# Block-sorted attention and a squared-ReLU FFN: half of the first q loaded in fp32 by SyncE and cast by ScalarE, with a new order of the work

## The chip, the cores and the metric

One core of a Trainium2 chip runs the whole kernel. The metric is the device time of one execution in microseconds; the median of three runs of the kernel before is 220.72 us (220.32 to 221.7).

## What is computed

There are 4 batches, 8 heads, 768 tokens and a head dimension of 64. The tokens of a head form 8 blocks of 96. A Sinkhorn iteration makes an 8x8 matrix P for each head, P mixes the blocks of k and of v, each block of q attends to its own mixed block, and a feed-forward layer follows.

```python
P = sort_net
for _ in range(5):
    P = exp(P - max(P, -1)); P = P / sum(P, -1); P = P / sum(P, -2)
k_sorted = einsum('bhij,bhjcd->bhicd', P, k_blocks)      # the same for v
attn = softmax(q_block @ k_sorted_block.T / sqrt(D))     # 96x96, block by block
x = (attn @ v_sorted_block)  as [3072 tokens, 512]
h = max(x @ w_in, 0)                                     # 512 -> 2048
out = (h * h) @ w_out                                    # 2048 -> 512
```

All inputs and the output are fp32; the kernel computes in bf16 with fp32 sums.

## The kernel before

**Stages.** A pair of heads (`hp`, 0 to 3) of a batch is one unit of attention, and half a batch (384 tokens) is one unit of the FFN, eight in all. A unit of attention goes through K and V (the sorts: k and v times the spread P, L593 and L629, evicted by L248 and L250), S (scores L664, then exp L684 or L693), T (a transpose of v, L713), A (product with v L855, then a reciprocal and a multiply on DVE, L865 and L866) and X (a transpose of the result into xT: on PE, L914, or as a DMA transpose on SP, L890). Batch 0 is done in two halves, so that the first FFN unit can begin early. An FFN unit is 64 up matmuls (L983; six of unit 0's are made ahead as single pieces, L941), a ReLU on ACT (L991), a square on DVE (L994), and 48 down matmuls (L1013, L1041) whose results go out through L962 on SP.

**Loads.** GpSimd (POOL) issues all loads of q, k, v and the weights, in one stream, and its DMAs turn fp32 into bf16 on the way (L320). Batch 0 comes first: all heads of q in two pieces of 64 partitions each (L351, L352), then k and v in turn for each pair, then w_in, w_out, and batch 1. SP loads only sort_net (L265). Batches 2 and 3 are loaded behind small copies on POOL (`hold`, L1130) that wait for xT of the batch before.

**The lead-in.** While the loads come, ACT and DVE run the five Sinkhorn rounds: an exp on ACT (L441), then sums, reciprocals and products on DVE (L398 to L402). PE runs matmuls on a tile of ones that nobody reads (`fill`, L427), 10 of them at the start (`warm`, L431), and others where the planner sees a gap. Between them PE transposes q of batch 0 (L543), and ACT copies the results into qT (L248); these copies stand in ACT's queue between the exps. At the end of the rounds p is spread over the partitions (L454), w_all is built from it (L466, on DVE and POOL), and the sorts begin.

**What sets the order.** The kernel writes its order by hand. Every step is an `Op` with an engine, a cost in us and its dependencies. `Plan.run` (L136) goes through them with these costs, and the instructions are recorded in the order that comes out; each engine runs its own in order. Two lists steer it: `FIRST` gives the order on PE for the first half of batch 0 (K0, v0 and so on; F0 to F7 are the FFN pieces made ahead; capitals are evicted by ACT, small letters by DVE, and a quote switches the PSUM buffer), and `DUES` gives, for each later step of attention, the number of FFN steps after which it is due on PE. DMA transfers are Ops of the pseudo-engines DMA and WAY, whose costs stand for the time on the way.

**v by way of DRAM.** From batch 1 on, v is sorted in another layout (L749), cast to `vn`, written to the DRAM buffer v_way by SP (L773) and read back as `vblk` (L779). k and q are turned by DMA transposes on SP (kx, L804; qz, L831). The DMA transposes of the second half of batch 0 (L890) wait for a POOL copy, the `gate` (L896), that waits for part 2 of w_out.

Of the kernel before, what the change touches and what calls it, by code (L numbers as in the profile page):

```python
# [8 lines left out]
FP32 = mybir.dt.float32  # L9
BF16 = mybir.dt.bfloat16  # L10
AF = mybir.ActivationFunctionType
ALU = mybir.AluOpType
# [6 lines left out]


DUES = {
    (0, "K"): (-266.0, -275.0, -427.5, -387.5),
    (0, "S"): (-233.0, -241.5, -349.0, -343.5),
    (0, "T"): (-217.0, -257.5, -368.5, -320.5),
    (0, "A"): (-107.5, -204.5, -291.0, -102.0),
    (0, "X"): (-11.0, -68.5, -149.5, -90.5),
    (0, "W"): (-274.5,),
    (1, "V"): (-104.0, -85.5),
    (1, "Q"): (-75.0,),
    (1, "N"): (None, -22.5),  # L30
    (1, "Z"): (None, None, -13.5, 11.0),
    (1, "S"): (-49.5, 0.0, 8.5, 49.0),
    (1, "A"): (-13.0, 2.0, 11.0, 50.5),
    (1, "X"): (42.0, 19.0, 38.5, 54.0),
    (2, "L"): (42.0,),
    (2, "N"): (57.5, 84.5),
    (2, "V"): (63.5, 76.0),
    (2, "Z"): (73.0, 73.0, 98.0, 88.0),
    (2, "S"): (90.5, 92.5, 100.5, 99.5),
    (2, "A"): (92.0, 93.5, 101.5, 100.0),  # L40
    (2, "X"): (99.0, 107.0, 110.0, 107.5),
    (3, "L"): (117.5,),
    (3, "N"): (122.5, 135.0),
    (3, "V"): (130.5, 141.0),
    (3, "Z"): (138.5, 146.5, 155.5, 153.5),
    (3, "S"): (148.5, 150.0, 161.5, 158.5),
    (3, "A"): (149.5, 154.0, 161.5, 159.5),
    (3, "X"): (155.5, 159.5, 236.5, 162.0),
}

FIRST = ("K0' v0 K1 v1 S0 t0 S1 t1' A0 K2 V2 A1 K3 S2 t2 v3 S3 x1 A2 T3' x0' A3 X2 F0 F1 F4 F6 "
         "F7 x3 F3")


class Op:
# [127 lines left out]
def kernel(  # L185
# [10 lines left out]
    nc = tc.nc  # L196
# [110 lines left out]
    w_in_bf = const.tile([128, KC, d_ff], BF16)  # L307
    w_out_bf = const.tile([128, NT, d_model], BF16)
    xT = const.tile([128, KC, n_tok], BF16)
    w_all = const.tile([128, H + HP, NB, C0], BF16)  # L310
    w_t = const.tile([128, NH // 4, 4, NB], BF16)
    qkv = {}
# [35 lines left out]

    first = plan.add("DMA", 4.55, lambda e: None)
    landed["last"] = first  # L350
    load(0, 0, 0, H, slice(0, 64))  # L351
    load(0, 0, 0, H, slice(64, 128))  # L352
    id_op = plan.add("POOL", 0.4, lambda e: make_identity(nc, ident, nomemset=True))
    mask = const.tile([128, C0], BF16)
    mask_t = const.tile([128, 4], BF16)
# [67 lines left out]
    def fill(us, slot):  # L423

        n = int(us / 0.24)
        for r in [4] * n + [2] * (us - 0.24 * n > 0.12):
            nc.tensor.matmul(  # L427
                out=p2[slot][:, 0, 0:128 * r].rearrange("p (r x) -> p r x", r=r), lhsT=ones,
                rhs=ones[:, None, :].to_broadcast([128, r, 128]), start=True, stop=True)

    def warm(e):  # L431
        fill(2.4, 0)


    plan.add("PE", 4.3, warm, [plan.add("DVE", 1.1, lambda e: None)])

    exps = []
    step = plan.add("SP", 2.25, lambda e: None)
    step0 = step
    for it in range(5):  # L440
        step = plan.add("ACT", 0.26, lambda e: nc.scalar.activation(  # L441
            out=p_sb, in_=p_sb, func=AF.Exp), [step])
        exps.append(step)
        if it == 0:
            plan.add("ACT", 0.6, make_sel, [step, id_op])
        step = plan.add("DVE", 0.66, lambda e: sink_norm(e, 0), [step])
        step = plan.add("DVE", 0.47 if it == 4 else 0.72, lambda e, it=it: sink_norm(e, 1, it == 4), [step])

# [81 lines left out]
    def s_q(b, hp, p0, p1, due=0, after=None, eng=AD):  # L530

        n = p1 - p0
        t = {}

        def mm(e):
            qb = qkv[b][0]
            if b == 0:
                t["p"] = psf.tile([128, NA, n], BF16, tag="pf", name="qtp")
            else:
                t["p"] = ps1.tile([128, NA, n], BF16, tag="p1", name="qtp")  # L540
            for a in range(NA):
                for h in range(2):
                    nc.tensor.transpose(  # L543
                        out=t["p"][64 * h:64 * (h + 1), a, :],
                        in_=qb[p0:p1, 2 * hp + h, D * a:D * (a + 1)],
                        identity=ident[p0:p1, p0:p1])
# [12 lines left out]

        if b == 0:  # L560
            dep = landed[b, 0, 0, p0]
        else:
            dep = landed[b, 0, HP * (2 * hp // HP), 0]
        ring = rf if b == 0 else r1
        s1, old = ring.take()
        if p0 == 0:
            qTs[b, hp], oldq = rqT.take()
        else:
            oldq = []
        pe = plan.add("PE", 0.04 + 0.0023 * n, mm, [dep, id_op] + old, due, mode="col")  # L570
# [314 lines left out]
    def s_xt(u, due=0, eng=AD, own=True):  # L885
        early = u.b == 0 and u.halves == (1,) and u.hp < HP - 1
        if early or u.b > 1 or u.b == 1 and u.hp < HP - 1:
            def turn(e):
                t0 = S * u.b + BLK * u.i0
                nc.sync.dma_start_transpose(  # L890
                    out=xT[:, u.hp, t0:t0 + BLK * u.ni].rearrange("p (n q) -> p n q", q=BLK),
                    in_=u.ao.rearrange("p n e d -> p (n e d)"))

            if early and "gate" not in holds:
                def gate(e):
                    nc.gpsimd.tensor_copy(out=xT[0:1, 0:HP - 1, HS:HS + 1],  # L896
                                          in_=w_out_bf[0:1, 3 * NT // 4 - HP + 1:3 * NT // 4, 0:1])

                holds["gate"] = plan.add("POOL", 0.1, gate, [landed["w_out", 2]])
            sp = plan.add("SP", 1.4, turn, u.norms + [holds["gate"]] * early)  # L900
            op = plan.add("WAY", 6.0 if early else 1.3, lambda e: None, [sp], tail=5.0 if early else None)
            rao.use(u.nao, op)
            for hf in u.halves:
                x_done[u.b, u.hp, hf] = op
            return
        st = {}

        ring = r1 if own else rf

# [281 lines left out]
```

## Time and profile before

| What | Value |
|---|---|
| median of 3 runs | 220.72 us |
| the profiled execution, its own time | 221.3 us |
| its span | 219.5 us |
| PE busy | 210.1 us (96%) |
| ACT, DVE, POOL busy | 120.8, 109.0, 28.5 us |
| up matmuls L983 | 506, 326 ns each |
| down matmuls L1013 | 352, 379 ns each |
| DMA | 31.52 MB, mean 144 GB/s |

The span is the time from the first to the last instruction in the profile. A row of the timeline gives the start and the duration in us, the engine, the line, the operation, out<-in and the count, and in brackets how long the engine sat idle before and what released it. PE is the matmul row and PEld the load of its weights. Matmuls are pipelined, so one shows 326 ns where the next follows after 163.

### The profile page before, as it was taken

To read this page: it belongs to the slowest core of one execution; us is meant where nothing else is said; L and a number is where in the kernel's file an instruction comes from. 1 tells how busy PE (TensorE), PEld (TensorE's weight loads), DVE (VectorE), ACT (ScalarE), POOL (GpSimd) and SP (SyncE) were. 2 spreads that over 40 slices of the span, in tenths; PEclk is the share of its full clock that TensorE was granted. 3 is DMA by queue.
4 is the path that set the end of the run, shared out by engine and by line. 5 is a ranking of instruction groups with operands and counts; after the bars stand their busy time and mean duration, and the time that the engine had idled before them with its cause. 6 is when DMAs were issued, how large, how long until landed. Compare 5 with 4: busy or idle time off the path is not lost.

```text
span 219.5 us, 5063 instructions
## 1 busy us (share of the span) xinstructions
PE 210.1 (96%) x2020; PEld 115.7 (53%) x2036; DVE 109.0 (50%) x298; ACT 120.8 (55%) x248; POOL 28.5 (13%) x53
## 2 busy tenths in 40 slices
PE   8998999979999999999989999999999999999994
PEld 2566765436555555445645455445655465456542
DVE  5777764245687437327666136426694155015300
ACT  4675885236875268326974168426866276147421
POOL 7994221000000510000000150000000000000000
PEclk9999999999999999999999999999999999999999
DMA  5999999999784599369974489689987310120012
GB/s 65 198 202 207 207 207 212 184 174 268 198 165 113 75 216 225 52 172 187 203 196 85 134 138 226 116 206 203 154 205 110 97 48 3 48 88 7 0 51 96
DMA packets 47831, 31.52 MB, mean 144 GB/s; under 512 B 27264, under 2 KB 42880, under 8 KB 47808
## 3 DMA queue, kind: packets, MB, share of 16 engines
q0 software_dynamic: 12736, 13.63, 38.5%
q1 hardware_dynamic: 35072, 17.56, 34.9%
q8 instruction: 16, 0.26, 0.5%
q14 instruction: 7, 0.06, 0.1%
HBM read 29.70 MB, written 8.72 MB: 175 GB/s over the span
## 4 chain that ended last, share of the span: by engine, by line
PE 79%; DMA 12%; POOL 4%; issue 1%; ACT 1%; DVE 1%; SPq 0%; POOLq 0%
PE hp L983 36%; PE op L1013 31%; DMA xT<-ao 5%; DMA w_in_bf<-in_moe_w_in_dram 5%; PE p L855 3%; PE p L664 3%; DMA vblk<-v_way 3%; PE op L1041 2%; PE p L749 1%; POOL kb L320 1%; POOL vb L320 1%; ACT h L991 1%; PE p L629 1%; DVE h L994 1%; PE hp L941 1%
## 5 line engine op out<-in xcount | busy, mean ns | idle before, releaser
L983 PE MATMUL hp<-xT,w_in_bf 128*128 128x384 bf16 x506 | 88.2, 326 | 1.5 <-DMA xT<-ao 1.5
L1013 PE MATMUL op<-w_out_bf,h 128*128 128x512 bf16 x352 | 82.9, 379 | 0.9 <-issue 0.2
L991 ACT ACTIVATE h<-hp 128x384 bf16<-128x384 f32 x128 | 62.1, 494 | 19.0 <-PE hp L983 16.2
L994 DVE TENSOR_TENSOR h<-h 128x384 bf16<-128x384 bf16 x128 | 43.8, 355 | 48.5 <-ACT h L991 48.1
L983 PEld LDWEIGHTS <-w_in_bf 128*128 128x128 bf16 x506 | 47.2, 98 | 33.3 <-DMA xT<-ao 2.0
L1013 PEld LDWEIGHTS <-h 128*128 128x128 bf16 x368 | 34.1, 98 | 38.0 <-issue 0.9
L248 ACT COPY ob<-op 128x512 f32<-128x512 f32 (+2 forms) x25 | 14.2, 568 | 50.6 <-PE op L1013 48.2
L693 ACT ACTIVATE et<-p 96x384 bf16<-96x384 f32 x48 | 19.9, 488 | 8.5 <-PE p L664 8.2
L866 DVE TENSOR_TENSOR ao<-p,rec 96x512 bf16<-96x512 f32 x32 | 22.0, 686 | 1.1
L855 PEld LDWEIGHTS <-et 96*128 96x128 bf16 x256 | 11.4, 97 | 6.5 <-ACT h L991 1.7
L865 DVE RECIPROCAL rec<-p 96x8 f32<-96x8 f32 x32 | 6.4, 202 | 13.0 <-PE p L855 12.1
L250 DVE CAST vn<-p 128x768 bf16<-128x768 f32 x6 | 5.7, 958 | 13.3 <-PE p L749 13.3
L1130 POOL COPY held<-xT 1x3 bf16<-1x3 bf16 (+1 forms) x2 | 0.4, 184 | 85.6 <-DMA xT<-ao 85.6
L855 PE MATMUL p<-vblk,et 96*128 96x65 bf16 x192 | 9.6, 193 | 1.3 <-DMA vblk<-v_way 1.3
L809 DVE COPY kvT<-kx 128x768 bf16<-128x768 bf16 x10 | 8.5, 848 | 4.7 <-DMA kx<-kn 4.7
L427 PE MATMUL p<-ones 128*128 128x512 bf16 (+1 forms) x28 | 9.3, 459 | 1.3 <-DVE ones L269 1.1
L664 PEld LDWEIGHTS <-kvT 64*128 64x128 bf16 x256 | 6.3, 94 | 5.9 <-issue 1.9
L248 ACT CAST vn<-p 128x768 bf16<-128x768 f32 x6 | 4.8, 799 | 5.9 <-PE p L749 5.9
L250 DVE CAST kn<-p 128x768 bf16<-128x768 f32 x5 | 4.8, 958 | 6.0 <-PE p L749 6.0
L320 POOL DMA_DIRECT2D kb<-in_k_dram x10 | 6.4, 644 | 4.4 <-DMA w_in_bf<-in_moe_w_in_dram 2.0
L320 POOL DMA_DIRECT2D vb<-in_v_dram x10 | 6.3, 632 | 4.0 <-DMA w_in_bf<-in_moe_w_in_dram 4.0
L320 POOL DMA_DIRECT2D qb<-in_q_dram x8 | 6.2, 770 | 4.6 <-DMA w_out_bf<-in_moe_w_out_dram 2.1
(80 smaller groups left out, 114.9 us busy)
## 6 DMA issues: line engine op xcount, KB each, us to landing
out_dram<-ob SPq DMA_DIRECT2D x23, 256.0 KB, 3.4
qb<-in_q_dram POOLq DMA_DIRECT2D x8, 384.0 KB, 11.7
v_way<-vn SPq DMA_DIRECT2D x6, 396.0 KB, 5.1
vblk<-v_way SPq DMA_DIRECT2D x6, 396.0 KB, 4.2
vb<-in_v_dram POOLq DMA_DIRECT2D x6, 384.0 KB, 12.0
kb<-in_k_dram POOLq DMA_DIRECT2D x6, 384.0 KB, 10.6
w_in_bf<-in_moe_w_in_dram POOLq DMA_DIRECT2D x4, 512.0 KB, 12.2
w_out_bf<-in_moe_w_out_dram POOLq DMA_DIRECT2D x4, 512.0 KB, 17.6
```

The source lines that it names most:

```text
L248: nc.scalar.copy(out=out, in_=in_)
L250: nc.vector.tensor_copy(out=out, in_=in_)
L320: nc.gpsimd.dma_start(out=dst, in_=src)
L427: nc.tensor.matmul(out=p2[slot][:, 0, 0:128 * r].rearrange("p (r x) -> p r x", r=r), lhsT=ones, rhs=ones[:, None, :].to_broadcast([128, r, ...
L664: nc.tensor.matmul(out=scp[:, h, BLK * n:BLK * (n + 1)], lhsT=u.ksT[64 * h:64 * (h + 1), HS * hf + BLK * n:HS * hf + BLK * n + 128], rhs=( ...
L693: nc.scalar.activation(out=et[:, h, 0:HS].rearrange("p (n c a) -> p n c a", c=C0, a=NA), in_=st["p"][0:96, h, 0:HS].rearrange("p (n a c) - ...
L855: nc.tensor.matmul(out=oup[:, h, 66 * n:66 * n + D + 1], lhsT=et_r[u.et[hf]][:, h, BLK * n:BLK * n + 128], rhs=(u.vs[:, NQ * hf + n, h, 0: ...
L866: nc.vector.tensor_tensor(out=u.ao[:, n0:n0 + NQ, :, :].rearrange("p n e d -> p e n d"), in0=ov[:, :, :, 0:D], in1=rec[:, :, :, None].to_b ...
L983: nc.tensor.matmul(out=t["hp", nt][:, 0:HS], lhsT=w_in_bf[:, kc, 128 * nt:128 * (nt + 1)], rhs=xT[:, kc, t0:t0 + HS], start=(kc == 0), sto ...
L991: nc.scalar.activation(out=t["h1", nt], in_=t["hp", nt][:, 0:HS], func=AF.Relu)
L994: nc.vector.tensor_tensor(out=t["h2"][:, nt, :], in0=t["h1", nt], in1=t["h1", nt], op=ALU.mult)
L1013: nc.tensor.matmul(out=t["op", mt], lhsT=t["h2"][:, nt, 128 * mt:128 * (mt + 1)], rhs=w_out_bf[:, nt, :], start=(nt == 0), stop=(nt == NT ...
```

## The change

q of heads 0 to 3 of batch 0 is no longer loaded by POOL. SP loads it in fp32, in two DMAs of two heads, right after sort_net, into a part of xT that is not yet used. ACT casts each into qb, behind exps 1 and 2. POOL's two q loads carry heads 4 to 7 only. The transposes of pairs 0 and 1 wait for the casts. Four instructions on constants are new, ahead of the fill on PE (two fp32 matmuls), on DVE (one multiply with a running sum, with a memset before it and a reciprocal after it) and on ACT (an exp whose scale is read from a tile). No output depends on them. All entries of `DUES` and the order in `FIRST` are new, and the time that the planner keeps a DMA transpose of xT in the second half of batch 0 busy on the way changes (`tail` from 5.0 to 3.8).

```diff
-    (0, "K"): (-266.0, -275.0, -427.5, -387.5),
+    (0, "K"): (-232.0, -238.5, -413.0, -404.5),
...
-    (1, "V"): (-104.0, -85.5),
-    (1, "Q"): (-75.0,),
+    (1, "V"): (-107.5, -57.0),
+    (1, "Q"): (-50.0,),
...
-FIRST = ("K0' v0 K1 v1 S0 t0 S1 t1' A0 K2 V2 A1 K3 S2 t2 v3 S3 x1 A2 T3' x0' A3 X2 F0 F1 F4 F6 "
-         "F7 x3 F3")
+FIRST = ("K0 v0 k1' S0 t0' v1 K2' k3 S1 A0 T1' V2' v3 S2 A1 T2' t3' S3 x0' A2 X1 F0 F1 A3 X2 F3 "
+         "F4 x3 F6 F7")
...
+    q32 = [xT[:, 1 + g, 2 * S:].bitcast(FP32).rearrange("p (h x) -> p h x", h=2)
+           for g in range(2)]
+    for g in range(2):
+        nc.sync.dma_start(out=q32[g], in_=q_r[0, :, 2 * g:2 * g + 2, :])
...
-    load(0, 0, 0, H, slice(0, 64))
-    load(0, 0, 0, H, slice(64, 128))
+    load(0, 0, HP, HP, slice(0, 64))
+    load(0, 0, HP, HP, slice(64, 128))
...
+    t32 = xT[:, 3, 2 * S:].bitcast(FP32)
+    nc.vector.memset(t32[:, 0:128], 1.0)
+    nc.vector.scalar_tensor_tensor(
+        out=t32[:, 128:136], in0=t32[:, 0:8], scalar=1.0, in1=t32[:, 8:16],
+        op0=ALU.mult, op1=ALU.mult, accum_out=t32[:, 136:137])
+    nc.vector.reciprocal(out=t32[:, 137:138], in_=t32[:, 136:137])
+
     def warm(e):
+        for n in (8, 16):
+            nc.tensor.matmul(out=p2[1][:, 0, 16 * n:17 * n], lhsT=t32[:, 0:128],
+                             rhs=t32[:, 0:n], start=True, stop=True)
         fill(2.4, 0)
 
+    def try_exp(e):
+        nc.scalar.activation(out=t32[:, 140:148], in_=p2[1][:, 0, 128:136], func=AF.Exp,
+                             scale=t32[:, 137:138])
...
         if it == 0:
+            plan.add("ACT", 0.4, try_exp, [step])
+        if it == 1:
             plan.add("ACT", 0.6, make_sel, [step, id_op])
+        if it in (1, 2):
+            def cast(e, g=it - 1):
+                alloc_qkv(0)
+                nc.scalar.copy(out=qkv[0][0][:, 2 * g:2 * g + 2, :], in_=q32[g])
+
+            casts.append(plan.add("ACT", 0.8, cast, [step, plan.add(
+                "WAY", 2.6 + 0.9 * it, lambda e: None, tail=2.6 + 0.9 * it)]))
...
-            dep = landed[b, 0, 0, p0]
+            dep = casts[hp] if hp < HP // 2 else landed[b, 0, HP, p0]
...
-            op = plan.add("WAY", 6.0 if early else 1.3, lambda e: None, [sp], tail=5.0 if early else None)
+            op = plan.add("WAY", 6.0 if early else 1.3, lambda e: None, [sp], tail=3.8 if early else None)
```

More of the change, by code (lines that the diff above doesn't have):

```diff
@@ L21 @@
 DUES = {
-    (0, "K"): (-266.0, -275.0, -427.5, -387.5),
[L23 to L27, printed above, removed]
-    (1, "V"): (-104.0, -85.5),
-    (1, "Q"): (-75.0,),
[L30 to L48, printed above, removed]
-}
-FIRST = ("K0' v0 K1 v1 S0 t0 S1 t1' A0 K2 V2 A1 K3 S2 t2 v3 S3 x1 A2 T3' x0' A3 X2 F0 F1 F4 F6 "
-         "F7 x3 F3")
+    (0, "K"): (-232.0, -238.5, -413.0, -404.5),
+    (0, "S"): (-204.0, -204.5, -355.5, -296.0),
+    (0, "T"): (-231.5, -163.5, -378.0, -266.0),
+    (0, "A"): (-198.0, -109.5, -291.0, -100.5),
+    (0, "X"): (-51.5, -27.5, -263.5, -74.5),
+    (0, "W"): (-288.5,),
+    (1, "V"): (-107.5, -57.0),
+    (1, "Q"): (-50.0,),
+    (1, "N"): (None, -39.5),
+    (1, "Z"): (None, None, 1.0, 47.5),
+    (1, "S"): (-40.5, -15.5, 11.5, 49.5),
+    (1, "A"): (-27.5, 2.5, 12.5, 51.5),
+    (1, "X"): (22.0, 6.0, 42.5, 54.5),
+    (2, "L"): (45.5,),
+    (2, "N"): (70.5, 75.5),
+    (2, "V"): (73.0, 79.0),
+    (2, "Z"): (79.5, 85.0, 93.5, 93.0),
+    (2, "S"): (80.0, 85.5, 99.5, 97.0),
+    (2, "A"): (80.0, 87.5, 101.0, 98.5),
+    (2, "X"): (89.5, 99.0, 125.0, 130.0),
+    (3, "L"): (130.5,),
+    (3, "N"): (130.5, 138.5),
+    (3, "V"): (132.0, 143.0),
+    (3, "Z"): (142.5, 143.0, 153.0, 145.0),
+    (3, "S"): (148.0, 148.5, 161.0, 157.0),
+    (3, "A"): (148.0, 156.5, 162.5, 157.5),
+    (3, "X"): (155.5, 165.0, 169.0, 183.5),
+}
+FIRST = ("K0 v0 k1' S0 t0' v1 K2' k3 S1 A0 T1' V2' v3 S2 A1 T2' t3' S3 x0' A2 X1 F0 F1 A3 X2 F3 "
+         "F4 x3 F6 F7")
 class Op:
@@ L429, in fill @@
                 rhs=ones[:, None, :].to_broadcast([128, r, 128]), start=True, stop=True)
+    t32 = xT[:, 3, 2 * S:].bitcast(FP32)
[4 more added lines that the diff above has]
+    nc.vector.reciprocal(out=t32[:, 137:138], in_=t32[:, 136:137])
     def warm(e):
+        for n in (8, 16):
+            nc.tensor.matmul(out=p2[1][:, 0, 16 * n:17 * n], lhsT=t32[:, 0:128],
+                             rhs=t32[:, 0:n], start=True, stop=True)
         fill(2.4, 0)
+    def try_exp(e):
+        nc.scalar.activation(out=t32[:, 140:148], in_=p2[1][:, 0, 128:136], func=AF.Exp,
+                             scale=t32[:, 137:138])
     plan.add("PE", 4.3, warm, [plan.add("DVE", 1.1, lambda e: None)])
-    exps = []
+    exps, casts = [], []
     step = plan.add("SP", 2.25, lambda e: None)
```

## The prediction

> **What bounds the kernel now.** I read the page first, then the waits of PE, the chain of work in order of time, the timeline of the first 23 us, and the windows of the same stretch.
>
> ```profile
> PE 210.1 (96%) x2020; PEld 115.7 (53%) x2036; DVE 109.0 (50%) x298; ACT 120.8 (55%) x248; POOL 28.5 (13%) x53
> ```
> PE is busy for 210.1 of 219.5 us, so only what PE waits for, or what stands before its useful work, can be won. The waits of PE (total, times, longest) name two stalls after the lead-in:
> ```profile
> PE hp L983 <- DMA xT<-ao: 1.5, 1, 1.5
> PE p L855 <- DMA vblk<-v_way: 1.3, 1, 1.3
> ```
> The chain (start, us, what) places them:
> ```profile
> 10.43 9.93 DMA w_in_bf<-in_moe_w_in_dram
> 20.36 0.05 issue
> 20.41 0.50 PE hp L941 x2
> ...
> 22.72 1.08 PE hp L983 x6
> ...
> 38.07 11.39 DMA xT<-ao
> 49.46 0.05 issue
> 49.51 2.12 PE hp L983 x12
> ...
> 110.04 5.55 DMA vblk<-v_way
> ```
> From 22.72 on PE does the same work in both kernels. So the end is: the time of that milestone (first L983, its six L941 pieces done), plus fixed work, plus stalls. The opening timeline (start, us, engine, line) shows what sets the milestone:
> ```profile
> 1.06 5.58 PE L427 MATMUL p<-ones 128*128 128x512 bf16 x15 [1.06 <-DVE ones L269]
> 1.25 1.52 POOL L320 DMA_DIRECT2D qb<-in_q_dram  x2 [0.80 <-POOLq L1175]
> 6.98 0.48 ACT L248 COPY qT<-qtp 128x384 bf16<-128x384 bf16 x1 [0.91 <-PE qtp L543]
> 7.58 0.26 ACT L441 ACTIVATE p_sb<-p_sb 32x64 f32<-32x64 f32 x1
> 16.17 0.27 PEld L593 LDWEIGHTS <-kb 128*64 128x64 bf16 x12 [0.35 <-DMA kb<-in_k_dram]
> 17.64 0.27 PEld L593 LDWEIGHTS <-vb 128*64 128x64 bf16 x12 [0.60 <-DMA vb<-in_v_dram]
> ```
> The sorts of pair 3 wait for kb at 16.17 and vb at 17.64, the first FFN piece for w_in at 20.41: until the milestone the load stream decides. Windows (DMA share and GB/s last) show when it starts:
> ```profile
> 3.50:4.00 0.50, 0.50 (x2) 0.15 (x1) 0.43 (x3) 0.31 (x1) 0.48 (x2) 1.00 0.55 48
> 4.00:4.50 0.50, 0.50 (x3) 0.20 (x2) 0.18 (x2) 0.26 (x1) 0.42 (x2) 1.00 1.18 177
> ```
> It is at speed only from about 4.0, and then holds about 200 GB/s of bf16, which is 0.4 MB of fp32 a microsecond.
>
> **What the Trainium skill says.** "DMA: Bandwidth & Descriptors", section "Issuing engines are not separate DMA queues": all issuers share the same 16 engines and another one saves issue time only. So the move buys an earlier start, not a higher rate; the trace of before agrees in so far as its stream is flat once it runs. "TensorE: Matmul & The Clock Gate", Part 1: the array runs at 1.2 GHz until about 3.4 us of sustained work, with N=512 matmuls 426.7 ns apart. The trace agrees on the pitch: weight loads of the fill stand 0.43 us apart up to 5.72. "FP8 and Floating Point Precision", TensorE Precision Notes: a true FP32 product takes four passes. No fp32 matmul is in this trace.
>
> **The change, part by part.**
>
> *Loads.* Half of q (4 heads, 4*128*384*4 B = 0.786 MB) leaves POOL's queue for SP's, right behind p_sb, whose issue at 0.74 took 0.40; p_sb landed 1.5 us after its issue. I put the first q bytes at 2.5 (estimate), and 0.786/0.4 = 2.0 us for them, so 4.5 for the end. Before, the same bytes went over 4.0 to 6.0. The rest of the stream moves up by 1.5 us. Lower bound 0 (same engines, slow start for HBM itself), upper 2.0 (all of it free). POOL still issues two q pieces, only of half the size, so its queue of k, v and weights issues when it did (kb 3.08, vb 5.43): early enough, as 1.573 MB of q last until 2.5+3.9 = 6.4. Arrivals become kb3 14.7, vb3 16.1, w_in 18.9.
>
> *Casts.* Two ACT casts of 128x768; nearest row, the 128x768 cast of vn: 0.80. ACT runs exps at 2.29, 4.05, 5.81, 7.58, 9.34, and between them is idle. Cast 0 goes behind sel: 4.31+0.62+0.80 = 5.73, just ahead of 5.81; cast 1 is 6.07 to 6.9. Cover: the DVE half of each Sinkhorn round. Both cost nothing while q has landed; behind them in ACT's queue stand exps 2 and 3, and so the whole Sinkhorn chain.
>
> *Trial instructions.* On DVE a memset, a scalar_tensor_tensor and a reciprocal, under 0.2 each by the rows of their neighbours, inside the 0.85 idle before 2.58: nothing. On ACT one Exp (0.26) in idle time before 4.05: nothing. On PE two fp32 matmuls stand ahead of all fill and wait for the last memset (et ends 1.73, this one about 1.9) in place of the first: PE starts 0.85 later. Their price is unknown. Below: two short bf16 ones, 0.1. Above: four passes with a weight load that reads four times as long, 2*4*0.43 = 3.4. I take eight passes of a cold load at 0.13 each: 1.0. Fill then starts near 2.9 instead of 1.06. The planner was not told (its costs for the fill are unchanged): in the program's order PE has 11 fills before the first q transposes, 4 behind them, and some 24.5 before the spread of p, against 24 now. With 11 fills at 0.43 (the last ones faster if the clock is up) the first transposes come at about 7.4, the ACT copy of qT at 7.8, and exp 3, which stands behind it, at 8.3 instead of 7.58. Exp 4 waits likewise for three more copies. The spread, now at 11.32, slips by about 0.8 (0 to 1.6).
>
> *Lead-in with the new order.* I walk K0 to X3 with durations of the rows: sort 0.2 (+0.4 to its eviction), ACT copy 0.48, exp 0.81, DVE copy 0.56, norm 0.9, T copies 0.42/0.58. With the spread on time: K0 12.03, S0 exp 13.4, K2 copy 14.5 (POOL's w_all is done at 14.05, behind its w_in issues), S1 exp 15.4 (kb3 at 14.7 stands ahead of S1 on PE), T1 16.2, V2 16.8, S2 exp 17.3, T2 18.1, S3 exp 18.7 to 19.5, A3 norm 20.1 to 21.0, X3 21.05, last pieces, 0.88 of L629 sorts: milestone 22.5. The spread 0.8 late costs only 0.1 of it, because POOL and kb3 give slack: 22.6. 1.5 late gives 23.2. I take 22.8, or +0.1, with a range of -0.2 to +0.8. So ACT, not the stream, becomes the limit, and the earlier loads are worth almost nothing here.
>
> *First stall.* The third transpose of xT was issued about 38, after a POOL gate on w_out part 2 (35.23); it now moves up with the stream by about 1.4, and lands near 48.1. In front of its user the new DUES also put 12 q transposes and 24 sorts (0.46+0.67 = 1.13). PE is then ready at 48.0+0.1+1.13 = 49.2: no wait. Gain 1.5.
>
> *Second stall.* The new order has batch 1's attention some 8 to 16 down-projection matmuls (0.22 each) earlier, so batch 2 loads earlier. The last attention product of pair 2 was at 69.2; from 48.1 I now add 1.13, 64 up-projection matmuls at 0.163 (10.4), 8 down (1.7) and about 4.0 for the k sorts, scores and products between: 65.3. The gate on the loads, 73.48 before, and all that hangs on it come some 3 us earlier. On SP the second v_way write stands one transpose earlier and the vblk read no longer behind two out_dram. The read, 110.04 before, comes at about 103 and lands near 108, and its user stands at 110. Gain 1.3. Batch 3 by the same walk keeps some 2 us of slack.
>
> *Sum.* -1.5 -1.3 +0.1 = -2.7; I keep 0.1 for waits that the walk misses: -2.6. The profiled execution took 221.3 for its span of 219.5, so span 216.9 and 218.7 for that execution. The median of the runs, 220.72, is 0.58 below the profiled one; the same 2.6 off it gives 218.1.
>
> **Rivals.**
> *One stall stays.* The vblk path has four steps (gate, load, write, read), each with its queue; if one is late, or a new wait of the size appears, only 1.5-0.1 is won: 219.4. For it: the write took up to 11.1 us to land. Against: 2 us of slack by the walk.
> *The transfer is hidden anyway.* If SP's bytes bring the stream no forward, kb3 stays at 16.2, and in the new order S1's exp stands behind it: milestone about 23.9, +1.2. Both stalls still shrink by the order: -2.8+1.2 = -1.6, or 219.1. Against: the stream idles before 4.0.
> *Slower: the fp32 pair at the head of PE.* If fill starts so late that the spread slips over 3.9 us, the milestone slips 2.9 (past 1.5 late it follows one to one) and eats both gains. With the 1.0 for 0.8 above, that needs a pair of over about 4 us; at 5, 222. Its upper price of 3.4 speaks against it. No other step holds up PE so early.
>
> **How the numbers follow.** Chances: forecast 0.60, one stall 0.18, hidden 0.15, slower 0.07. A measurement of this kernel tells about 1%, 2.2 us, from no change, so faster means under 218.5. The forecast, 217.2 to 218.9 on its own bounds, is under it 8 times in 10 (0.48); the others add 0.04: faster 0.52. Slower by over 1% only at the far end of the last: 0.05. Same 0.43. The range for 8 in 10 reaches from 217.0 to the rivals at 220.2.
>
> **What would show it.** Right: packets of q on the hardware queue before 3 us; POOL's stream ahead by about 1.5 (w_in landing near 18.9); casts that end before 5.81 and 7.58; no PE wait on xT<-ao near 49 and none on vblk; the milestone between 22.5 and 23.5. Wrong: a cast that waits for q and holds exp 2; the pair lasting over 2 us; a new PE wait in batch 1, where the write of v has to come back sooner than before.

## The result, and the profile after

| | before | after |
|---|---|---|
| median | 220.50 us (17 runs) | 219.57 us (17 runs, 219.0 to 220.41) |
| ratio | | 0.9951, 95% interval 0.9934 to 0.9968 |
| profiled execution, its own time | 221.3 us | 219.84 us |
| its span | 219.5 us | 218.1 us |

The change gains 1.1 us by the ratio (0.0049 * 220.5), within 1%. The forecast was 2.6. The time lies inside the range, but 1.5 above the predicted value. The ratios here and below leave out executions over 1.5% above the fastest of the same kernel, which the medians keep; only for short_fill does this matter. First the page's line of busy times and the waits of PE (total, times, longest):

```profile
PE 209.6 (96%) x2024; PEld 116.3 (53%) x2041; DVE 111.0 (51%) x303; ACT 121.9 (56%) x250; POOL 28.3 (13%) x53
```
```profile
PE p L444 <- DVE xT L436: 1.9, 1, 1.9
PE tp L620 <- DMA kb<-in_k_dram: 0.6, 1, 0.6
PE p L882 <- DMA vblk<-v_way: 0.6, 1, 0.6
```
Both stalls that headed the list before, 1.5 on xT<-ao and 1.3 on vblk, are gone. In their place stand a wait of 0.6 on kb in the lead-in, and a new one of 0.6 on vblk. (L882 and L1010 are the lines L855 and L983 of before.) The chain of work in order of time shows where they are:

```profile
8.86 7.56 DMA kb<-in_k_dram
16.42 0.04 issue
16.46 0.40 PE tp L620 x12
...
23.15 0.88 PE p L656 x48
24.03 1.08 PE hp L1010 x6
...
41.67 12.68 DMA v_way<-vn
54.41 4.67 DMA vblk<-v_way
...
59.13 0.67 PE p L882 x16
```
The milestone (first up matmuls after the six early pieces) comes at 24.03 instead of 22.72. The third row says why: pair 3's k sort starts at 16.46, as its load lands (16.42), where the prediction had 14.7. The new vblk wait is in batch 1, and ends at 59.13. PE ends at 214.51 (before 216.30). The opening timeline shows the parts of the change:

```profile
1.21 0.92 SPq L313 DMA_DIRECT2D xT<-in_q_dram  x2
1.92 1.04 PE L444 MATMUL p<-xT 128*128 128x8 f32 x4 [1.92 <-DVE xT L436]
2.80 4.30 PE L431 MATMUL p<-ones 128*128 128x512 bf16 x11
4.80 0.83 ACT L469 CAST qb<-xT 128x768 bf16<-128x768 f32 x1
6.52 0.83 ACT L469 CAST qb<-xT 128x768 bf16<-128x768 f32 x1 [0.37 <-DMA xT<-in_q_dram]
7.82 0.25 ACT L459 ACTIVATE p_sb<-p_sb 32x64 f32<-32x64 f32 x1
12.80 0.36 PE L481 MATMUL pt_ps<-p_ij,xT 32*128 32x32 bf16 x8
```
The fp32 pair holds PE from 1.92 to 2.80, then the fill begins. The second cast waits for SP's second load, which landed at 6.50. The spread comes at 12.80; before it came at 11.32.

The windows from 8 to 14 us, of before and then of after, have the rate of the load stream in their last column (GB/s written; the two columns before it are PE's clock and the DMA share):

```profile
8.00:14.00 6.00, 5.89 (x134) 3.48 (x132) 4.66 (x20) 4.60 (x13) 6.00 (x9) 1.00 1.30 198
```
```profile
8.00:14.00 6.00, 5.77 (x130) 3.31 (x129) 3.47 (x17) 3.79 (x11) 5.19 (x8) 1.00 1.25 178
```
The stream was flat at 198 before; it runs at 178 after. Kb of pair 0 landed 0.67 earlier than before (8.50 against 9.17), v of pair 0, the next load, no earlier (10.32 against 10.33), and kb of pair 3 0.29 later (16.42 against 16.13).

**Where the time went.** Windows from the milestone to PE's end give 193.58 us before and 190.48 after. So the span's -1.4 adds up like this: milestone +1.31, xT stall -1.51, vblk stall -1.28, new vblk wait +0.56, the rest of PE's work -0.87, and from PE's end to the span's end +0.39 (3.20 before, 3.59 after).

The -0.87 is for the most part busy time. In these two windows PE has 1642 matmuls in both kernels, and is busy for 189.71 before and 188.70 after, 1.01 less; its idle time apart from the three named waits is 0.14 more. The mean time of one matmul is the same (up 326 ns, down 379, products 193 in both), so the difference lies in how they follow one another. Which neighbour makes it was not tried.

The +0.39 comes with the move of q. In the traces of all eight kernels below that load q on SP, 3.6 pass from the end of PE's last matmul to the end of the span (3.57 to 3.61); in all six with q on POOL, 3.2 (3.20 to 3.25). The records of SP's semaphore instructions show how. At the end SP waits for the semaphores of its DMAs in the order of their numbers, one about 0.06 after the other, and its DMAs take these semaphores in turn. Before, the last output has the highest number (118), and the waits for the others are done when it lands, 1.9 after PE's end. SP's two more loads shift the turn: in after the last output has number 109, lands 1.9 after PE's end as well, and six more waits stand behind it.

### The profile page after: what moved, and what is told of

It reads as the page before. It is cut to its first block, busy times and chain, and to the rows that moved or that the text cites. A ratio compares the mean times of both kernels' runs of the same rounds, so it can differ in the third digit from the quotient of the medians.

```text
span 218.1 us, 5074 instructions
## 1 busy us (share of the span) xinstructions
PE 209.6 (96%) x2024; PEld 116.3 (53%) x2041; DVE 111.0 (51%) x303; ACT 121.9 (56%) x250; POOL 28.3 (13%) x53
## 4 chain that ended last, share of the span: by engine, by line
PE 78%; DMA 11%; POOL 3%; DVE 3%; issue 1%; ACT 1%; POOLq 0%; DVEq 0%; SPq 0%
PE hp L1010 34%; PE op L1040 33%; DMA v_way<-vn 6%; DMA kb<-in_k_dram 3%; PE p L882 3%; PE p L691 3%; DMA vblk<-v_way 2%; PE op L1068 2%; PE p L776 1%; DVE ao L893 1%; POOL vb L324 1%; POOL kb L324 1%; PE p L656 1%; ACT h L1018 1%; DVE h L1021 1%
## 5 line engine op out<-in xcount | busy, mean ns | idle before, releaser
L1010 PE MATMUL hp<-xT,w_in_bf 128*128 128x384 bf16 x506 | 87.8, 326 | 0.0
L1010 PEld LDWEIGHTS <-w_in_bf 128*128 128x128 bf16 x506 | 47.5, 98 | 31.4 <-issue 0.5
L248 ACT COPY ob<-op 128x512 f32<-128x512 f32 (+2 forms) x24 | 13.6, 568 | 47.1 <-PE op L1040 44.7
L882 PEld LDWEIGHTS <-et 96*128 96x128 bf16 x256 | 11.4, 97 | 5.3 <-DMA vblk<-v_way 0.9
L882 PE MATMUL p<-vblk,et 96*128 96x65 bf16 x192 | 9.3, 193 | 0.6 <-DMA vblk<-v_way 0.6
L711 ACT ACTIVATE et<-p 96x768 bf16<-96x768 f32 x8 | 6.3, 807 | 1.4 <-PE p L691 1.4
## 6 DMA issues: line engine op xcount, KB each, us to landing
kb<-in_k_dram POOLq DMA_DIRECT2D x6, 384.0 KB, 10.5
```

The costliest lines, as they stand in the source:

```text
L248: nc.scalar.copy(out=out, in_=in_)
L882: nc.tensor.matmul(out=oup[:, h, 66 * n:66 * n + D + 1], lhsT=et_r[u.et[hf]][:, h, BLK * n:BLK * n + 128], rhs=(u.vs[:, NQ * hf + n, h, 0: ...
L1010: nc.tensor.matmul(out=t["hp", nt][:, 0:HS], lhsT=w_in_bf[:, kc, 128 * nt:128 * (nt + 1)], rhs=xT[:, kc, t0:t0 + HS], start=(kc == 0), sto ...
```

## Experiments

Each was timed beside the kernel before. "Milestone" is the chain's figure (the timeline's is 0.07 lower; k3_later and old_first have only that one). "kb 3 landed" is the load of k of pair 3, "GB/s" the rate written from 8 to 14 us. All columns from the spread on are of one profiled execution each.

| kernel | ratio [95%] | median | spread | kb 3 landed | k sort of pair 3 | milestone | GB/s |
|---|---|---|---|---|---|---|---|
| before | 1 | 220.5 | 11.32 | 16.13 | 16.18 | 22.72 | 198 |
| after | 0.9951 [0.9934, 0.9968] | 219.57 | 12.80 | 16.42 | 16.46 | 24.03 | 178 |
| no_trials | 0.9973 [0.9950, 0.9996] | 219.46 | 12.19 | 16.46 | 16.50 | 24.23 | 176 |
| q_pool_frozen | 0.9942 [0.9920, 0.9963] | 219.08 | 13.80 | 16.50 | 16.6 | 24.23 | 200 |
| q_move_alone | 1.0060 [1.0040, 1.0081] | 221.6 | 12.24 | 15.89 | 16.55 | 22.86 | 178 |
| order_alone | 1.0335 [1.0312, 1.0357] | 227.58 | 11.33 | 16.10 | 16.37 | 24.10 | 200 |
| old_first | 1.0107 [1.0074, 1.0141] | 222.77 | 13.41 | 16.64 | 17.75 | 23.88 | 167 |
| k3_later | 0.9968 [0.9951, 0.9985] | 219.82 | 12.89 | 16.71 | 16.76 | 23.61 | 170 |
| short_fill | 0.9991 [0.9959, 1.0023] | 222.09 | 13.72 | 15.39 | 16.6 | 24.55 | 179 |
| masks_late | 0.9926 [0.9901, 0.9950] | 218.71 | 13.12 | 14.68 | 16.0 | 23.55 | 200 |
| masks_late_nt | 0.9914 [0.9897, 0.9930] | 218.67 | 11.85 | 15.19 | 15.24 | 22.96 | 201 |
| masks_late_qpool_nt | 0.9932 [0.9916, 0.9949] | 219.06 | 12.46 | 16.09 | 16.14 | 23.86 | 202 |
| masks_late_before | 0.9991 [0.9980, 1.0002] | 220.2 | 11.52 | 15.88 | 15.93 | 22.57 | 201 |
| trials_on_before | 0.9993 [0.9966, 1.0020] | 220.62 | 13.08 | 16.47 | 17.38 | 23.73 | 200 |

Two things help to read it. First, the rate: the six kernels with q on SP and POOL's masks in their old place have 167 to 179, the other eight 198 to 202. A single landing varies more than that (short_fill's 15.39 is early at 179). Second, the spread: it also moves with the time at which PE's clock rises, which the fills show (one every 0.43 us, then about one every 0.22). Fills that begin at 2.80 are slow until about 6.2 in after, 7.0 in masks_late, 7.5 in trials_on_before and 8.4 in q_pool_frozen, so differences of some tenths between two spreads are not all due to the edit.

**no_trials: the four trial instructions taken out of the changed kernel, order frozen.**

```diff
-    t32 = xT[:, 3, 2 * S:].bitcast(FP32)
...
     def warm(e):
-        for n in (8, 16):
-            nc.tensor.matmul(out=p2[1][:, 0, 16 * n:17 * n], lhsT=t32[:, 0:128],
-                             rhs=t32[:, 0:n], start=True, stop=True)
         fill(2.4, 0)
...
-            plan.add("ACT", 0.4, try_exp, [step])
+            plan.add("ACT", 0.4, lambda e: None, [step])
```


> The changed kernel without its four trial instructions (nothing that the output needs is left out); the planner still sees their costs, so the order is the same. Theory A (the arrival of kb3, which stands ahead of S1 on PE, decides the lead-in): the fill starts at 1.06 and the spread comes back from 12.8 to about 11.5, but PE still waits for kb of pair 3 until about 16.4, so the milestone (first of the 500 up matmuls after the early pieces) stays within 0.3 of 24.0 and the time within 0.3 of 219.6. Rival B (the late start of the fill and with it the late spread decide): the milestone comes at 22.9 to 23.3 and the time falls by 0.7 to 1.1, to about 218.7.

The fill starts at 1.06 again, but the spread only returns to 12.19, not to 11.32, and the time is that of after (the intervals overlap). The timeline of no_trials shows what stands in for the pair:

```profile
5.77 0.38 PE L556 MATMUL qtp<-ident,qb 64*64 64x64 bf16 x12 [0.56 <-ACT qb L455]
6.82 0.83 ACT L455 CAST qb<-xT 128x768 bf16<-128x768 f32 x1 [0.67 <-DMA xT<-in_q_dram]
7.70 0.76 PE L556 MATMUL qtp<-ident,qb 64*64 64x64 bf16 x36 [0.58 <-ACT qb L455]
```
PE, now earlier, waits twice for a cast, 1.14 together, and the second cast waits for SP's load. So without any trial the spread is still 0.87 later than before, behind these waits; with the pair it is 0.6 later again. And neither counts here: kb of pair 3 is what the milestone waits for, at 16.50 as at 16.46.

**q_pool_frozen: q by POOL again, casts gone, everything else in the order of after.**

```diff
-    for g in range(2):
-        nc.sync.dma_start(out=q32[g], in_=q_r[0, :, 2 * g:2 * g + 2, :])
...
-            return qkv[b][t][p, h0:h0 + n, :], (q_r, k_r, v_r)[t][b, p, h0:h0 + n, :]
+            hs = slice(0, H) if (b, t) == (0, 0) else slice(h0, h0 + n)
+            return qkv[b][t][p, hs, :], (q_r, k_r, v_r)[t][b, p, hs, :]
...
-                nc.scalar.copy(out=qkv[0][0][:, 2 * g:2 * g + 2, :], in_=q32[g])
```


> The changed kernel, instruction for instruction in its own order on every engine, but all heads of q come through POOL's two loads again; SP's q loads and ACT's two casts are gone. Theory A (the q move is worth nothing in the new order, because pair 3 of k and v and w_in do not come earlier for it): kb3 reaches PE near 16.2, the milestone stays at 23.8 to 24.3 and the time within 0.4 of the changed kernel. Rival C (the new order lives on the q move): kb3 at 16.7 or later, the milestone past 24.7, 0.7 or more slower.

It is no slower than after: 219.08, though its spread is another 1.0 later (13.80). The stream is back at 200 GB/s from 8 to 14:

```profile
8.00:14.00 6.00, 6.00 (x113) 3.11 (x107) 2.98 (x15) 3.90 (x10) 5.43 (x8) 1.00 1.31 200
```
Kb of pair 0 lands at 9.23 here and at 8.50 in after, kb of pair 3 at 16.50 and 16.42. So the move of q brings nothing in the changed kernel: what the stream gains by it at the head it loses again on the way.

**q_move_alone: the order of before, q by SP with the casts, no trials.**

```diff
+    for g in range(2):
+        nc.sync.dma_start(out=q32[g], in_=q_r[0, :, 2 * g:2 * g + 2, :])
...
-    load(0, 0, 0, H, slice(0, 64))
-    load(0, 0, 0, H, slice(64, 128))
+    load(0, 0, HP, HP, slice(0, 64))
+    load(0, 0, HP, HP, slice(64, 128))
...
+                nc.scalar.copy(out=qkv[0][0][:, 2 * g:2 * g + 2, :], in_=q32[g])
```


> The kernel before with half of q loaded by SP in fp32 and cast by ACT, in the old order, without the trial instructions. Theory A (the loads of pair 3 and w_in do not come earlier for it): kb3, vb3 and w_in reach PE within 0.4 of 16.2, 17.6 and 20.4, milestone 22.5 to 22.9, both old stalls stay (1.5 on xT, 1.3 on vblk), time within 0.4 of the kernel before. Rival D (the stream moves up by 0.8 to 1.5 and only this one profile lost it): kb3 at 15.4 or earlier, w_in by 19.5, milestone 21.6 to 22.2, time lower by up to 0.9.

Slower, by 0.4 to 0.8%. The stream runs at 178 GB/s here too, and kb of pair 3 landed only 0.24 earlier than before (15.89). Its sort, at 16.55, did not wait for it, so that time says nothing on the load. Two vblk waits of 2.2 together appeared later; the planner is told of the casts and of the loads and shifts other steps too, so they are not evidence on the move.

**order_alone: the kernel before with the new DUES, FIRST and tail, and nothing else.**

```diff
-    (0, "K"): (-266.0, -275.0, -427.5, -387.5),
+    (0, "K"): (-232.0, -238.5, -413.0, -404.5),
...
-FIRST = ("K0' v0 K1 v1 S0 t0 S1 t1' A0 K2 V2 A1 K3 S2 t2 v3 S3 x1 A2 T3' x0' A3 X2 F0 F1 F4 F6 "
+FIRST = ("K0 v0 k1' S0 t0' v1 K2' k3 S1 A0 T1' V2' v3 S2 A1 T2' t3' S3 x0' A2 X1 F0 F1 A3 X2 F3 "
```

> The kernel before with the new DUES, FIRST and tail, all of q loaded by POOL, no trial instructions. Theory A (the q move is worth next to nothing by kb3, the order brings all the gain): kb3 near 16.2, milestone 23.7 to 24.0, no wait on xT near 49, time 219.2 to 219.8. Rival C (the q move brings what the lead-in has, the order alone starves): kb3 at 16.5 or later and the milestone past 24.5, time over 220.2.

Much slower, by waits of 4.7 on xT<-ao (3.6 of it in one, that ends at 129.8). The planner derives another later order from the same lists when the lead-in's costs differ, so the new lists only fit the kernel that they were written with. Up to the milestone the kernels are comparable: there it shows the new FIRST with an early spread (11.33) and kb landed at 16.10, as before, and the milestone is 24.10 against 22.72. So with q loaded as before, the new FIRST alone costs the lead-in 1.38; in it pair 3's k sort stands ahead of S1. The spread was not what held the milestone in after.

**old_first: the changed kernel with FIRST of before.**

```diff
-FIRST = ("K0 v0 k1' S0 t0' v1 K2' k3 S1 A0 T1' V2' v3 S2 A1 T2' t3' S3 x0' A2 X1 F0 F1 A3 X2 F3 "
-         "F4 x3 F6 F7")
+FIRST = ("K0' v0 K1 v1 S0 t0 S1 t1' A0 K2 V2 A1 K3 S2 t2 v3 S3 x1 A2 T3' x0' A3 X2 F0 F1 F4 F6 "
+         "F7 x3 F3")
```

> The changed kernel with the FIRST of before; DUES, q move, trial instructions and tail as changed. Theory A (the new FIRST, which puts kb3 in front of S1 and A0 on PE, costs the lead-in 1.2, and the new DUES bring the whole gain behind it): milestone 22.8 to 23.2, no wait on xT near 49, time 218.2 to 218.8. Rival F (the lead-in is late with either order, as the spread is): milestone 23.7 or later, time 219.3 or more.

The milestone comes at 23.88 with this order as well, as the spread is late (13.41; trials_on_before has the same FIRST, 13.08 and 23.73). Later waits (xT 1.8, vblk 0.6) then make it slower, again with an order that the planner shifted. So what the new DUES bring with FIRST of before and an early spread is in no run.

**k3_later: pair 3's k sort moved behind T1 in FIRST, its v sort behind S2; later order as in after.**

```diff
-FIRST = ("K0 v0 k1' S0 t0' v1 K2' k3 S1 A0 T1' V2' v3 S2 A1 T2' t3' S3 x0' A2 X1 F0 F1 A3 X2 F3 "
+FIRST = ("K0 v0 k1' S0 t0' v1 K2' S1 A0 T1' k3 V2' S2 v3 A1 T2' t3' S3 x0' A2 X1 F0 F1 A3 X2 F3 "
```


> The changed kernel with only the sorts of k of pair 3 moved on PE behind S1, A0 and T1, and those of v of pair 3 behind S2. Theory A: S1, A0 and T1 no longer wait for kb3, the milestone comes at 23.2 to 23.6 and the time falls by 0.4 to 0.8. Rival G (pair 3 itself, whose v comes last, sets the end of the lead-in): milestone within 0.2 of 24.0, same time.

The milestone comes 0.35 earlier (23.61 against 23.96 by the timelines), as S1 no longer stands behind the late load; the time does not move. The gain is gone before PE's next up matmuls: they start at 50.29 (50.28 in after), as the last transpose of xT has just landed, at 50.25. Then the waits of PE show:

```profile
PE p L882 <- DMA vblk<-v_way: 0.9, 1, 0.9
```
It is the batch-1 wait, 0.9 instead of 0.6: PE is no earlier there, and the read of v landed at 59.44 instead of 59.08.

**short_fill: four fills at the start instead of ten, the pair kept.**

```diff
-        fill(2.4, 0)
+        fill(0.96, 0)
```


> The changed kernel with 4 fill matmuls at the start in place of 10, so that the fp32 pair stays at the head of PE but what comes behind it is on time. Theory A: spread about 11.5, kb3 as before near 16.4, time within 0.3 of the changed kernel. Rival B: as without the trials, 0.7 to 1.1 faster. If the shorter fill leaves PE at its slow clock for longer, matmuls of the lead-in have twice their pitch up to about 10 and the gain of B is halved.

This is not a kernel without the pair's delay. In its trace the clock of PE rises later: four fills that take 1.04 in after take 1.89 here, fills are slow until 10.5, and the spread slips to 13.72. Of its 22 runs seven lie from 219.0 to 219.7, twelve from 222.0 to 222.9 and three between, so its median says little; the profiled execution (219.65) belongs to the lower group. The Trainium skill, "TensorE: Matmul & The Clock Gate", Part 1, says that the window that decides on the clock runs free, so that the number of slow matmuls differs from run to run; the clock's rise differs between the traces here too (see below the table). Whether it makes the two groups is not shown, as no trace of a slower run was taken.

**masks_late: POOL's six mask operations behind its last load of k and v.**

```diff
             nc.gpsimd.dma_start(out=dst, in_=src)
+            if key == (0, 2, 2 * HP - 2, 0):
+                make_mask(e)
...
-    plan.add("POOL", 1.5, make_mask, [id_op])
+    plan.add("POOL", 1.5, lambda e: None, [id_op])
```


> The changed kernel with the six mask operations of POOL moved from ahead of its second load to behind its last k and v load, so that v of pair 0 is issued at 3.7 in place of 5.3 and the loads behind it 1.6 earlier; nothing else moves. Theory S (after the q move the stream runs short of work, because POOL hands it the loads too late): the early lead of 0.8 is kept, kb3 reaches PE by 15.7, the milestone comes at 23.2 to 23.5, and the time falls by 0.5 to 0.8. Rival E (the engines lose the lead by themselves): kb3 within 0.3 of 16.4, same time.

In after, POOL spends 3.69 to 5.33 on the masks, between its first and second k/v load. The timelines of POOL, after and then masks_late:

```profile
2.95 0.73 POOL L324 DMA_DIRECT2D kb<-in_k_dram  x1
...
5.27 0.74 POOL L324 DMA_DIRECT2D vb<-in_v_dram  x1
```
```profile
2.94 0.73 POOL L324 DMA_DIRECT2D kb<-in_k_dram  x1
3.66 0.74 POOL L324 DMA_DIRECT2D vb<-in_v_dram  x1
```
With the loads handed over 1.6 earlier the stream runs at full rate, in the window from 8 to 14 of masks_late:

```profile
8.00:14.00 6.00, 5.77 (x113) 3.08 (x112) 3.45 (x16) 3.85 (x12) 5.00 (x11) 1.00 1.31 200
```
The loads now land when the prediction had them: kb and vb of pair 3 at 14.68 and 16.35 and the first part of w_in at 18.75, against 14.7, 16.1 and 18.9. PE waits for no load any more, the milestone is 23.55 in spite of a spread at 13.12, and the time is 218.71. The span is 1.2 under that of after: 0.5 by the milestone, and 0.7 where batch 1's read of v lands at 57.83 instead of 59.08 and PE no longer waits for it. The packets say the same of the stream: of POOL's packets that start in this window, nearly all of 768 bytes last 79 ns in every kernel, but 42 of 1453 last over 120 ns in after (up to 1.3 us), 8 of 1622 before, 2 of 1660 in masks_late, 1 of 1660 in q_pool_frozen. So here the loss needs both: q on SP, which brings the k/v stream forward, and loads handed over as late as before. Which amount of lead would be enough was not tried.

**masks_late_nt: the same without trial instructions.**

```diff
+            if key == (0, 2, 2 * HP - 2, 0):
+                make_mask(e)
...
-            nc.tensor.matmul(out=p2[1][:, 0, 16 * n:17 * n], lhsT=t32[:, 0:128],
-                             rhs=t32[:, 0:n], start=True, stop=True)
...
-            plan.add("ACT", 0.4, try_exp, [step])
+            plan.add("ACT", 0.4, lambda e: None, [step])
```

> The changed kernel with the six mask operations on POOL behind the last load of k and v (as in masks_late) and without the four trial instructions; order unchanged. Theory (the milestone is the later of the spread plus 10.4 and pair 3's k sort on PE plus 7.6): the spread comes at 12.2 as in the kernel without trials, pair 3's k sort at about 15.2 to 15.7, so the milestone at 22.7 to 23.3 against 24.03 after, no new wait of PE beyond those of masks_late, time 0.4 to 1.0 under masks_late's, about 218.0. If the trial instructions cost nothing even when the loads are no limit, it is equal to masks_late within 0.2 and the milestone stays at 23.5.

The spread is 11.85, the k sort 15.24, the milestone 22.96, as expected; the time, 218.67, is that of masks_late and not the 0.4 to 1.0 below it. The timelines of masks_late and then masks_late_nt show where the 0.6 is given back:

```profile
57.91 0.66 PE L884 MATMUL p<-vblk,et 96*128 96x65 bf16 x16
```
```profile
57.92 0.67 PE L870 MATMUL p<-vblk,et 96*128 96x65 bf16 x16 [0.43 <-DMA vblk<-v_way]
```
Both start batch 1's product at 57.9, when vblk has landed. What the lead-in wins beyond that point is waited away. This kernel has the lowest median here, and is faster than both that were given: 0.9914 [0.9897, 0.9930] of before, 0.4% under after by medians.

**masks_late_qpool_nt: the last kernel, with q by POOL and without casts.**

```diff
-        nc.sync.dma_start(out=q32[g], in_=q_r[0, :, 2 * g:2 * g + 2, :])
...
+            hs = slice(0, H) if (b, t) == (0, 0) else slice(h0, h0 + n)
...
-                nc.scalar.copy(out=qkv[0][0][:, 2 * g:2 * g + 2, :], in_=q32[g])
```

> The same (masks behind the loads, no trial instructions, order of the changed kernel), but q is loaded by POOL in two pieces again and the two casts are gone: the difference to the kernel above is what the move of q itself is worth once POOL hands its loads over in time. Theory: the stream was already full here, so pair 3's k sort stands at 15.9 to 16.3, the spread at 11.3 to 11.8, milestone 23.5 to 24.0, time 0.4 to 1.0 over the kernel above. Rival (the move is worth nothing under any supply, transfers share one rate): the same milestone and time as above within 0.2.

With the loads handed over in time, moving q is worth 0.90 in the k sort (16.14 against 15.24) and in the milestone (23.86 against 22.96). The lead of 0.85 lasts to PE's last matmul (213.28 against 214.13). Then the end of SP, described above, takes 0.34 of it back (3.59 against 3.25), so 0.51 is left in the span. The medians differ by 0.4 (219.06 against 218.67; the intervals overlap, but the slowest of the four runs above, 218.81, is under the fastest of these five, 218.94).

**masks_late_before: the kernel before with the masks late.**

```diff
+            if key == (0, 2, 2 * HP - 2, 0):
+                make_mask(e)
...
-    plan.add("POOL", 1.5, make_mask, [id_op])
+    plan.add("POOL", 1.5, lambda e: None, [id_op])
```

> The kernel before with the six mask operations behind the last load of k and v, and nothing else. Theory: POOL was ahead of the stream there (flat at 0.2 MB a microsecond from 5 on), so handing over earlier brings nothing: pair 3's k sort stays at 16.0 to 16.2, milestone 22.5 to 22.8, time within 0.3 of before. Rival (the mask operations held up the stream in the kernel before as well): k sort at 15.0 to 15.5, milestone down by 0.5 or more, time down by as much.

Within 0.2% of before: where q is all on POOL, its stream did not suffer from the masks.

**trials_on_before: the kernel before with the four trial instructions, plan and order unchanged.**

```diff
+    t32 = xT[:, 3, 2 * S:].bitcast(FP32)
+    nc.vector.memset(t32[:, 0:128], 1.0)
...
     def warm(e):
+        for n in (8, 16):
+            nc.tensor.matmul(out=p2[1][:, 0, 16 * n:17 * n], lhsT=t32[:, 0:128],
+                             rhs=t32[:, 0:n], start=True, stop=True)
         fill(2.4, 0)
...
+            if it == 0:
+                try_exp(e)
```

> The kernel before with the four trial instructions and nothing else: order and plan unchanged, q by POOL. Theory: the fp32 pair holds the fill back by about 0.9, the spread slips from 11.3 by 0.8 to 1.6, but there the loads decide and the slack takes most of it: milestone 22.7 to 23.1, time 0 to 0.4 over before. Rival (the order of before has no slack for a late spread): milestone and time later by the whole slip, 0.9 or more.

The spread slips by 1.76 and the milestone by 1.01, more than I expected, and the time doesn't move. Its timeline and its wait on xT (total, times, longest):

```profile
2.80 5.67 PE L427 MATMUL p<-ones 128*128 128x512 bf16 x15
8.40 0.76 PE L561 MATMUL qtp<-ident,qb 64*64 64x64 bf16 x36
```
```profile
PE hp L1001 <- DMA xT<-ao: 0.8, 1, 0.8
```
Before, the fill began at 1.06 and the transposes at 6.57; everything on PE up to the spread is 1.74 to 1.83 later. But the stall on xT shrinks from 1.5 to 0.8, as the transpose lands when it did: after the gate PE is only 0.3 behind (49.81 against 49.51). Here the stall that ended with a DMA swallowed a delay of PE ahead of it. The wait of 1.3 on vblk is missing from this trace as well: the read was issued at 109.64 and landed at 114.24, before at 110.04 and 115.59. So its span, 218.4, is 1.1 shorter than that of before, while the medians agree.

## Why the prediction missed, point by point

**Both stalls go: right in size, and one of them for another reason.** -1.51 and -1.28 were measured against -1.5 and -1.3. For vblk of batch 2 the walk said that the read comes at about 103; it was issued at 104.68, now ahead of two out_dram as the walk had it, before at 110.04, and PE found it landed. For xT the prediction said that the third transpose "now moves up with the stream by about 1.4, and lands near 48.1", with PE there at 49.2. The gate went at 35.42 (35.23 before), so the transpose did not move up: it was issued at 38.3, and the longest of the three took 11.7, so it landed near 50.0. The stall went because PE came later, at 50.28: the milestone's slip and the sorts and transposes in front. In masks_late_nt the sentence holds as written: gate at 34.21, transpose at 37.0 plus 11.4, 48.4, and PE's next up matmuls at 49.20 with no wait.

**The lead-in: the walk was right and both its inputs were wrong.** This is where the prediction failed: "+0.1" for the milestone, measured +1.31, outside its range of -0.2 to +0.8. The step that failed is "early enough", POOL's hand-over of k and v, and with it the arrival of pair 3's k: 14.7 forecast, 16.42 measured. In the new order the milestone is the later of two sums, as the table shows: spread + 10.4 (masks_late 13.12 to 23.55, q_pool_frozen 13.80 to 24.23), and k sort of pair 3 + 7.6 to 7.7 (after 16.46 to 24.03, no_trials, order_alone, masks_late_nt, masks_late_qpool_nt). In masks_late and q_pool_frozen PE waits for no k or v of pair 3, so the k sort follows the spread. Only short_fill is 0.4 over the later sum. The walk had "1.5 late gives 23.2", and 12.80 + 10.4 is 23.2; for masks_late, whose loads land as forecast and whose spread is 1.8 late, it gives 23.5, and 23.55 was measured. So of the 1.2 that the milestone misses its 22.8 by, the late spread is 0.4 and the late load 0.8. The inputs:

- "The rest of the stream moves up by 1.5 us." It moved up 0.67 at its head, and by pair 3's k it was behind the kernel before: 16.42, not 14.7. I had checked POOL's issues against the rates ("early enough, as 1.573 MB of q last until 2.5+3.9 = 6.4") and found them in time; SP's q did last until 6.5 and POOL's until 7.5. The conclusion was wrong: with the same loads issued 1.6 earlier the rate is restored, kb of pair 3 lands at 14.68 (masks_late), and the k sort comes at 15.24 where the spread is early (masks_late_nt). That the next transfer had been issued before the last one ended was not enough to hold the rate.
- "4.5 for the end" of SP's q. The first of two loads landed at 4.38, the second at 6.50, as POOL's q ran beside it from 3.7 on. The page cited in the prediction, "DMA: Bandwidth & Descriptors", says in "Queues, rings and completion order" that an engine takes turns between queues packet by packet; the trace agrees: of SP's q, 0.43 MB start from 3 to 5 us and 0.25 MB from 5 to 7, among POOL's packets. The prediction gave SP's bytes the whole rate. So cast 1 ran at 6.52 and not at 6.07, and "cost nothing" was wrong: in no_trials PE waits 1.14 for the two casts, and the spread is 0.87 later than before.
- The fp32 pair: priced at 1.0, took 0.88. But the slip of the spread, "about 0.8 (0 to 1.6)", came to 1.48 in after and to 1.76 where nothing else changed (trials_on_before). I followed it through exp 3, which was only 0.24 late (7.82). What counts is PE's own queue: all fills stand ahead of the spread in program order, so a fill that begins 1.74 later ends 1.74 later, less what PE would have waited. In after 1.14 of these 1.74 replace waits for the casts, and 0.6 comes on top of no_trials. The clock of PE, which rose at different times, is in these figures too. The trace has four records for the two matmuls, where I counted eight passes; together they took 0.88.

**"-2.7; I keep 0.1 for waits that the walk misses."** The new wait of 0.56 on vblk in batch 1 was among the things named as possibly wrong. It was paid for by -0.87 that I had excluded ("PE does the same work in both kernels") and followed by the +0.39 at SP's end, not foreseen. These three cancel, so the miss in the span is the milestone: +1.21 of 1.2.

**From the span to the median.** The prediction took the same 2.6 off the median of the runs. The profiled execution of before was 0.8 above its median (221.3 against 220.5), that of after 0.27; so of 1.46 between the profiled executions, 0.93 is left between medians. masks_late_nt has a span 2.6 shorter than that of before, the predicted sum, and a median only 1.8 lower. So the forecast took its stalls from one of the longer executions of before: 15 of the 17 runs are under 221.3. Other traces of its order point the same way. masks_late_before shows the stalls again (1.6 and 1.2), in the slowest of its 22 runs (221.18, median 220.20); trials_on_before, profiled 0.43 under its median, has 0.8 and none. That the stalls are shorter in most executions would follow, but is not shown: trials_on_before is another kernel, and no second trace of before was taken.

**The rivals.** "The transfer is hidden anyway" named the right place, k3 at 16.2 and a milestone about 23.9 (measured 16.46 and 24.03), and 219.1. It has the place and the size, for a partly different reason: SP's bytes did bring the stream forward, and then the stream ran slower. I gave it 0.15, as the stream idles before 4.0; it did, and that was not enough. "One stall stays" (219.4) was near in time by luck: both stalls went, and a new wait of 0.56 and the late milestone took their place. The slower rival did not come: the pair was under its limit of 4 us, and what it would have cost would have been partly swallowed, as trials_on_before shows.

**Chances.** 0.43 for no change by over 1%: that is what happened.

## What to carry to other kernels

Moving a load to a second queue paid here only where the first queue's later transfers were also issued earlier: look at the rate over the whole stretch behind the moved load, not only at its start. Two queues share the engines from the moment that both have packets, so give each its part of the rate. A gain or a delay counted only up to the next wait that ended with a DMA: before adding up a lead-in and two stalls, ask of each whether it is timed by PE or by the transfer, and whether the profiled execution is a typical one. And look behind PE's last matmul: two loads more on SP cost 0.36 at the end of the span.

## What was not expected of the hardware

- SP's first load of q was issued from 1.21 to 1.62, and its first packets started at 2.27, 0.65 after the issue had ended. "DMA: Bandwidth & Descriptors", "Latency and other measured facts", gives about 0.6 us for this path, which agrees if it is counted from the end of the issue.
- The stream of POOL's loads lost a tenth of its rate (178 against 198 to 200 GB/s) for 6 us while four or more of its loads were issued and not landed (kb of pair 3: issued 8.86, landed 16.42). It showed as single packets that lasted up to 1.3 us among ones of 79 ns. That it goes with q on SP together with loads issued late is shown, in six kernels against eight; what holds those packets is not.
- The slow fills before PE's clock rises were 0.43 us apart. Where they began at 1.06, this lasted until about 4.0 in no_trials and order_alone, 5.7 in before and 6.2 in masks_late_before; where they began at 2.80, until between 6.2 and 8.4 (10.5 in short_fill, with less fill). So the start of the work alone does not set the rise.
